# One DMA transpose of 1024 columns, or two of 512, in a recurrent attention and gated feed-forward kernel

## The chip, the core and the metric

The kernel runs on one core of a Trainium2 chip. The metric is the device time of one execution in microseconds (us). The engines named below are PE (TensorE: matmuls; PEld is its weight load), DVE (VectorE), ACT (ScalarE), POOL (GpSimd) and SP (SyncE, which here only issues DMAs). "SPq" is SP's queue of DMA issues: the time that SP spends on issuing.

## What is computed

Two stages, the second fed by the first. The first is a gated linear recurrence for each of 4 batches and 8 heads, over 768 positions with heads of 48:

```python
for t in range(S):
    state = alpha[:, :, t, :, None] * state + np.einsum('bhd,bhe->bhde', k[:, :, t], v[:, :, t])
    y[:, :, t] = np.einsum('bhd,bhde->bhe', q[:, :, t], state)
```

The second takes `x`, the output y with its heads side by side, 3072 rows of 384, and computes

```python
h = x @ w_in            # 384 -> 2048
g = h * np.cos(h)
return g @ w_out        # 2048 -> 384
```

Inputs and output are float32; the kernel multiplies in bfloat16.

## The kernel before

The 3072 rows are cut into 24 chunks of 128 positions, 6 for each batch. A chunk j goes through the recurrence in its parallel form: the logarithms of alpha are summed along the chunk by matmuls (`cums`, L162), the exponentials scale k and q (`scaled`, L208, by POOL or DVE) into the tile `kqb`, of which there are three slots, k in its first half and q in its second. Each half has 8 heads padded to 64 columns, so 512 columns a half and 1024 in all. Then k and q are transposed, so that the head's dimension lies along the partitions, into the tile `qkT` (128 partitions x 8 blocks x 128): blocks 0 to 3 hold k, 4 to 7 hold q, two heads a block. Scores (`scores`, L238) multiply blocks of both halves; a mask is applied (`mask_scores`, L246, on DVE); the state is updated (`state` L253, `ev_state` L260); outputs y come from scores and state (`outputs`, L275). The state matmuls read `kqb` itself, not its transpose.

The transpose has two forms. Chunks 0 to 8 use PE (`transposes`, L223) with a copy by DVE (`ev_transposes`, L231). Chunks 9 to 23 use a DMA transpose issued by SP (`transposes_dma`, L218 to L221): one instruction for all 1024 columns. `qkT` has six buffers.

The feed-forward stage of a chunk starts with y transposed too: on PE for some chunks (`x_transposes`, L300), by a DMA transpose of 384 columns on SP for 16 of them (`x_transposes_dma`, L296 to L298). Then come `ff1` (L313, 48 matmuls into `h_ps`), cosine on ACT (`act`, L323), the gate on DVE (`gate`, L329), `ff2` (L334) and a store.

The order of the work is written out by hand: one string, `ORDER` (L390), lists units such as `X17` (DMA transpose of chunk 17) or `K17` (k of chunk 17 scaled by POOL; `KD17` by DVE; `Q` and `QD` for q), and each unit emits its instructions on its engine in that order. Each engine works through its own list in order and waits for semaphores where it depends on others. So SP's list fixes the order in which loads of alpha, q, k and v (L111, L119), the weights, both kinds of transposes (L220, L298) and 16 of the 24 stores (L351) are issued; the other 8 stores are issued by ACT. Loads run ahead of their use by up to six chunks (`PF`).

In `ORDER` the transposes stand among the other units like this:

```python
"e7 A11 W9 k13 y10 E5 D10 et8 X12 u10 m11 eC8 eI8 Y11 A12 B10 st5 q13 v14 v12 G10 q15 yA11 D11 m12 B11 "
"V13 eI10 k18 u15 Y15 P_13 eC10 X16 bD16 x14 E9 A16 ss10 q18 S16 F14 m16 yA15 f_14 G14 X17 W13 Y16 QD18 "
"ss9 g_14 p_14 x15 e12 F15 a11 P_14 A17 yA16 W14 K18 bA17 uD16 V14 q19 m17 f_15 Y17 p_15 X18 A18 l11 G15 "
```

Of the kernel before, what the change touches and what calls it, by code (L numbers as in the profile page):

```python
# [16 lines left out]
def kernel(  # L17
# [10 lines left out]
    nc = tc.nc  # L28
# [5 lines left out]
    NP = H // 2  # L34
# [167 lines left out]
    def kq(j):  # L202
        return kqb[:, kq_slot.setdefault(j, len(kq_slot) % 3)]
# [13 lines left out]

    def transposes_dma(j):  # L218
        t = work.tile([C, 2 * NP, C], BF, tag="qkT", bufs=QB, name="qkT")
        nc.sync.dma_start_transpose(out=t, in_=kq(j).rearrange("s i h d -> s (i h d)"))  # L220
        qkT_t[j] = t  # L221

    def transposes(j):  # L223
# [138 lines left out]
    def on(f, *args):  # L362
# [12 lines left out]
        "K": on(scaled, 0, pool), "KD": on(scaled, 0, dve), "Q": on(scaled, 1, pool), "QD": on(scaled, 1, dve),  # L375
        "b": on(vcast, pool), "bA": on(vcast, act_e), "bD": on(vcast, dve),
        "X": transposes_dma, "T": transposes, "t": ev_transposes,
        "A": scores, "m": mask_scores, "S": state, "u": on(ev_state, pool), "uD": on(ev_state, dve),
        "Y": outputs, "y": on(ev_outputs, dve), "yA": on(ev_outputs, act_e),
# [71 lines left out]
```

## Time and profile before

| | |
|---|---|
| three runs | 192.05, 195.76 and 197.65 us; median 195.76 us |
| the profiled execution | 192.98 us, of which the span of the instructions is 191.3 us |
| granted TensorE clock | full in all 40 slices of the span |
| instructions | 5593 |
| matmuls of `ff1` (L320) and `ff2` (L340) | 70.3 and 69.7 us of PE's busy time, which overlaps itself |
| DMA transposes on SP | 15 of k and q (L220), 16 of y (L298) |
| DMA traffic | 35.74 MB in 117048 packets, mean 187 GB/s |
| SP's DMA queue (q1) | 115872 packets, 33.83 MB |
| ACT's DMA queue (q10) | 1152 packets, 1.57 MB, 8 stores |

The profile is one execution. A busy share of an engine is an average over the span. Lines of the timeline have the start and duration in us, the engine, the line of the kernel and the operation (out<-in); "x2" merges two neighbours, and brackets hold the idle time before the instruction and what ended it. "DMA to landing" is the time from the start of the issue on SP to the arrival of all data. In a window's DMA rows a digit is the mean busy share of the core's 16 DMA engines in a slice, in tenths, and GB/s is what they moved in it. Row "PE x ... [0.82 <-DVE g_sb L332]" reads: PE had nothing to do for 0.82 us, ended by DVE's result.

### The profile page before, as it was taken

What the parts mean: (1) busy time and instruction counts of PE and PEld (TensorE: products, weight loads), DVE (VectorE), ACT (ScalarE), POOL (GpSimd) and SP (SyncE); (2) the same over time, 40 slices, a digit from 0 to 9 for tenths busy, and PEclk for the clock granted to TensorE, in tenths of its full rate; (3) what the DMA queues carried; (4) which work ended last, traced back from release to release, by engine and by line L of the source; (5) the groups of instructions that cost most, each with busy time, mean ns of one, the idle gap of its engine ahead of it and who ended that gap; (6) DMA issues with size and microseconds to landing.
All of it is one profiled execution on the core that took longest, in us unless ns stands there. A gap on an engine that the chain in (4) does not pass through costs nothing.

```text
span 191.3 us, 5593 instructions
## 1 busy us (share of the span) xinstructions
PE 179.5 (94%) x2380; PEld 134.3 (70%) x2380; DVE 136.5 (71%) x181; ACT 119.7 (63%) x150; POOL 56.4 (30%) x85
## 2 busy tenths in 40 slices
PE   7988789999979999999999999899989999999992
PEld 2435568887758687887698858586857868877771
DVE  5024998888859787578768875877678978685371
ACT  2146588662768875458786988888676536326341
POOL 5042334135916130860246123402022244110000
PEclk9999999999999999999999999999999999999999
DMA  6999999999999896999999999989999998612122
GB/s 141 206 233 208 258 313 286 343 335 166 234 222 175 207 207 120 213 154 197 201 245 146 218 129 213 150 180 183 202 212 181 158 232 165 150 21 64 42 82 82
DMA packets 117048, 35.74 MB, mean 187 GB/s; under 512 B 110368, under 2 KB 115488, under 8 KB 117024
## 3 DMA queue, kind: packets, MB, share of 16 engines
q1 hardware_dynamic: 115872, 33.83, 88.4%
q10 hardware_dynamic: 1152, 1.57, 2.4%
q8 instruction: 18, 0.29, 0.7%
q14 instruction: 6, 0.05, 0.1%
HBM read 25.17 MB, written 4.72 MB: 156 GB/s over the span
## 4 chain that ended last, share of the span: by engine, by line
PE 67%; DMA 8%; SPq 8%; DVE 6%; ACT 4%; issue 3%; POOL 2%; DVEq 0%; POOLq 0%; ACTq 0%
PE o_ps L340 26%; PE h_ps L320 23%; PE w_ps L360 6%; SPq L220 4%; DMA qkT<-kqb 3%; PE A_ps L243 3%; DMA k_sb<-in_k_dram 2%; SPq L119 2%; DMA q_sb<-in_q_dram 2%; PE cum L167 2%; DVE g_sb L332 2%; SPq L298 2%; PE y_ps L285 2%; POOL kqb L210 2%; PE y_ps L282 1%
## 5 line engine op out<-in xcount | busy, mean ns | idle before, releaser
L326 ACT ACTIVATE c_sb<-h_ps,halfpi 128x1024 bf16<-128x1024 f32 x48 | 53.4, 1113 | 39.6 <-PE h_ps L320 38.0
L332 DVE TENSOR_TENSOR g_sb<-h_ps,c_sb 128x1024 bf16<-128x1024 f32 x48 | 58.5, 1220 | 19.4 <-ACT c_sb L326 18.5
L320 PE MATMUL h_ps<-xT,w 128*128 128x128 bf16 x1152 | 70.3, 219 | 0.7 <-DVE xT L309 0.4
L340 PE MATMUL o_ps<-w,g_sb 128*128 128x384 bf16 x384 | 69.7, 326 | 0.0
L320 PEld LDWEIGHTS <-w 128*128 128x128 bf16 x1152 | 65.8, 98 | 3.9 <-issue 0.6
L340 PEld LDWEIGHTS <-g_sb 128*128 128x128 bf16 x384 | 34.9, 98 | 21.0 <-issue 1.0
L248 DVE TENSOR_TENSOR A_sb<-A_ps,mask_f 128x1024 bf16<-128x1024 f32 x24 | 29.3, 1221 | 7.2 <-PE A_ps L243 7.1
L210 POOL TENSOR_TENSOR kqb<-k_sb,icpl 128x384 bf16<-128x384 f32 x18 | 18.6, 1034 | 22.8 <-DMA k_sb<-in_k_dram 10.6
L145 ACT ACT_TABLE_LOAD x18 | 23.1, 1283 | 1.1 <-PEq L435 0.8
L268 POOL TENSOR_TENSOR ub<-sc,Em 128x384 bf16<-128x384 f32 x10 | 8.6, 862 | 42.5 <-DVE sc L265 42.5
L210 POOL TENSOR_TENSOR kqb<-q_sb,cpl 128x384 bf16<-128x384 f32 x15 | 15.0, 1001 | 20.7 <-DMA q_sb<-in_q_dram 20.6
L360 PE MATMUL w_ps<-warm 128*128 128x512 bf16 x60 | 15.8, 406 | 1.3 <-DVE warm L58 1.3
L184 ACT ACTIVATE icpl<-cum 128x768 f32<-128x768 f32 (+1 forms) x13 | 10.0, 766 | 6.9 <-PE cum L167 6.9
L152 ACT ACTIVATE lnab<-a_sb 128x768 bf16<-128x768 f32 x12 | 10.2, 851 | 3.8 <-DMA a_sb<-in_alpha_dram 3.7
L184 ACT ACTIVATE cpl<-cum 128x768 f32<-128x768 f32 (+1 forms) x13 | 9.9, 762 | 3.7 <-PE cum L174 3.7
L210 DVE TENSOR_TENSOR kqb<-q_sb,cpl 128x384 bf16<-128x384 f32 x9 | 5.5, 607 | 9.0 <-ACT cpl L184 8.0
L285 PE MATMUL y_ps<-vpb,A_sb 128*128 128x48 bf16 x192 | 11.2, 183 | 0.4 <-DVE A_sb L248 0.4
L360 PEld LDWEIGHTS <-warm 128*128 128x128 bf16 x60 | 5.8, 103 | 7.9 <-issue 2.1
L285 PEld LDWEIGHTS <-A_sb 128*128 128x128 bf16 x192 | 9.7, 96 | 1.9 <-DVE A_sb L248 0.8
L243 PE MATMUL A_ps<-qkT 48*128 48x128 bf16 x192 | 9.5, 218 | 1.4 <-DVE A_sb L248 0.6
L282 PE MATMUL y_ps<-ub,qkT 128*128 128x96 bf16 x80 | 9.7, 204 | 0.6 <-POOL w L104 0.5
L265 DVE TENSOR_TENSOR sc<-U_ps,ub 128x384 f32<-128x384 f32 x16 | 8.8, 549 | 1.9 <-PE U_ps L257 1.9
(51 smaller groups left out, 132.3 us busy)
## 6 DMA issues: line engine op xcount, KB each, us to landing
q_sb<-in_q_dram SPq DMA_DIRECT2D x24, 192.0 KB, 4.7
a_sb<-in_alpha_dram SPq DMA_DIRECT2D x12, 384.0 KB, 4.9
k_sb<-in_k_dram SPq DMA_DIRECT2D x24, 192.0 KB, 4.7
v_sb<-in_v_dram SPq DMA_DIRECT2D x24, 192.0 KB, 4.3
w1f<-in_moe_w_in_dram SPq DMA_DIRECT2D x4, 768.0 KB, 6.9
w2f<-in_moe_w_out_dram SPq DMA_DIRECT2D x4, 768.0 KB, 9.1
out_dram<-o_sb SPq DMA_DIRECT2D x16, 192.0 KB, 2.9
out_dram<-o_sb ACTq DMA_DIRECT2D x8, 192.0 KB, 3.0
```

The source lines that it names most:

```text
L145: act_e.preload_act_table_set(nm)
L184: act_e.activation(out=d[g][:, c : c + n], in_=cum_of(g)[:, c : c + n, 0:HD], func=AF.Exp, scale=scale)
L210: eng.tensor_tensor(out=kq(j)[:, which, :, 0:D], in0=d.pop(j), in1=s[j // 2][:, j % 2].rearrange("s (h d) -> s h d", h=H), op=ALU.mult)
L243: nc.tensor.matmul(t[:, ACOL[h]], qkT_t[j][rows, h // 2], qkT_t[j][rows, NP + h // 2], start=True, stop=True)
L248: dve.tensor_tensor(out=t, in0=A_ps.pop(j), in1=mask_f.unsqueeze(1).to_broadcast([C, H, C]), op=ALU.mult)
L282: nc.tensor.matmul(t[:, 2 * p : 2 * p + 2], qT[:, NP + p], ub_t[prev(j)][:, p], start=True, stop=False, skip_group_check=True)
L285: nc.tensor.matmul(t[:, h], A[:, ACOL[h]], vp(j)[:, h], start=f, stop=True, skip_group_check=True)
L320: nc.tensor.matmul(t[:, f], w1[:, kk, ft * C : (ft + 1) * C], x_t[j][:, kk], start=(kk == 0), stop=(kk == 2))
L326: act_e.activation(out=t, in_=h_ps[j, half], func=AF.Sin, bias=halfpi, scale=1.0)
L332: dve.tensor_tensor(out=t, in0=h_ps.pop((j, half)), in1=c_t.pop((j, half)), op=ALU.mult)
L340: nc.tensor.matmul(o_ps[j][:, 0:DM], g_t[j, half][:, f], w2[:, half * HF + f], start=(o_n[j] == 0), stop=(o_n[j] == NF - 1))
L360: nc.tensor.matmul(w_t[0], warm[:, 0:C], warm, start=True, stop=True)
```

## The change

Each DMA transpose of scaled k and q is issued as two: k's 512 columns into blocks 0 to 3 of `qkT`, then q's 512 into blocks 4 to 7. Both are issued by SP, one right after the other, at the place in SP's list where the one stood. `ORDER` isn't touched, and the transposes of y and those on PE are as before. Each half waits for its own operand; the matmuls of the scores wait for both.

```diff
     def transposes_dma(j):
         t = work.tile([C, 2 * NP, C], BF, tag="qkT", bufs=QB, name="qkT")
-        nc.sync.dma_start_transpose(out=t, in_=kq(j).rearrange("s i h d -> s (i h d)"))
+        for i in range(2):
+            nc.sync.dma_start_transpose(out=t[:, i * NP : (i + 1) * NP], in_=kq(j)[:, i].rearrange("s h d -> s (h d)"))
         qkT_t[j] = t
```

## The prediction, made before the changed kernel ran

> **What bounds the kernel now.** I read the page first, then the idle time of PE, then the order of time on SP's queue, then the DMA rate in short windows.
>
> ```profile
> PE 179.5 (94%) x2380; PEld 134.3 (70%) x2380; DVE 136.5 (71%) x181; ACT 119.7 (63%) x150; POOL 56.4 (30%) x85
> PE 67%; DMA 8%; SPq 8%; DVE 6%; ACT 4%; issue 3%; POOL 2%; DVEq 0%; POOLq 0%; ACTq 0%
> ```
>
> PE is the bound, but the chain leaves PE for 16% of the span and runs through SP's queue and its transfers. The rows of PE in order of time show where that surfaces:
>
> ```profile
> 121.34 0.50 PE L167 MATMUL cum<-lnab,tri 64*128 64x384 bf16 x4 [0.82 <-DVE g_sb L332]
> 141.68 0.50 PE L167 MATMUL cum<-lnab,tri 64*128 64x384 bf16 x4 [0.67 <-DVE g_sb L332]
> 153.38 0.40 PE L243 MATMUL A_ps<-qkT 48*128 48x128 bf16 x8 [0.32 <-DMA qkT<-kqb]
> ```
>
> From 60 to 185 us the named idle time of PE is only these 1.8 us. The first goes back to a load: DVE waited 1.51 us for k of chunk 17, which SP issued at 114.23. So PE has almost nothing to win, and loses as soon as SP is late. SP's queue around that place:
>
> ```profile
> 107.79 4.45 SPq L220 DMA_TRANSPOSE qkT<-kqb  x2
> 112.34 1.21 SPq L298 DMA_TRANSPOSE xT<-y_sb  x1
> 113.60 0.57 SPq L119 DMA_DIRECT2D q_sb<-in_q_dram  x1
> 114.23 0.57 SPq L119 DMA_DIRECT2D k_sb<-in_k_dram  x1
> 114.85 2.34 SPq L119 DMA_DIRECT2D v_sb<-in_v_dram  x2
> 117.23 0.80 SPq L119 DMA_DIRECT2D k_sb<-in_k_dram  x1
> 118.13 3.15 SPq L220 DMA_TRANSPOSE qkT<-kqb  x1
> 121.38 1.20 SPq L298 DMA_TRANSPOSE xT<-y_sb  x1
> ...
> 123.78 1.42 SPq L220 DMA_TRANSPOSE qkT<-kqb  x1
> ```
>
> Start and duration stand in front. One instruction follows another within 0.1 us. From 57 to 165 us all of SP's gaps over 0.2 us add up to about 4 us (the largest at 60.6, 79.4, 143.1 and 162.9). This queue issues every load, transpose and most stores in a fixed order, so a longer instruction makes all behind it later.
>
> Its durations hold two things. The groups of the two transposes:
>
> ```profile
> L220 SPq DMA_TRANSPOSE qkT<-kqb x15: 1382/1933/3420, 67.6 to 161.4; - x15
> DMA to landing us min/median/max: 3.3/4.4/6.0
> L298 SPq DMA_TRANSPOSE xT<-y_sb x16: 1179/1202/2120, 61.8 to 174.3; - x16
> DMA to landing us min/median/max: 2.3/2.7/4.9
> ```
>
> Three blocks of 128 columns cost 1.18 us at least, eight cost 1.38: (1.38 - 1.18) / 5 = 0.04 us a block over a fixed 1.06. The cost is nearly all fixed, and the change pays it twice. What lies above 1.4 is mostly not a wait for data: the POOL rows end k of chunk 13 at 97.4 and of 16 at 116.1, well before 99.98 and 118.13 where their transposes begin and take 3.42 and 3.15 us. (The table of waits puts some of it down to POOL and DVE writing other chunks.) It is a queue waiting to drain: from 98 to 102 the DMA engines moved 203 to 238 GB/s with a backlog. I call these drain-limited. The third view, 85 to 90 us in 40 slices:
>
> ```profile
> DMA  9999999970000999999999999999999997799999
> GB/s 309 302 297 292 265 178 119 59 23 17 16 18 18 215 287 289 261 256 263 263 258 264 215 190 182 188 178 188 262 258 289 284 180 138 143 160 132 197 203 241
> ```
>
> The transpose of chunk 11 is issued at 85.87; the engines are empty until slice 13 (86.6), then move at about 260 GB/s. So 0.75 us of the fixed part pass before the first byte.
>
> **The change, part by part.**
>
> *Issue on SP.* Fifteen instructions of 8 blocks become thirty of 4. One half costs 1.06 + 4 x 0.04 = 1.22; I take 1.25, with a gap of 0.08 before the next (the rows' gaps are 0.05 to 0.10), so 2.58 for a pair. Against the undisturbed single of 1.38 to 1.59 this is +1.0 to +1.2. Against the drain-limited singles (2.18 to 3.42; chunks 10, 13, 14, 15, 16, 18, 19) it is +0 to +0.4, since the second fixed part passes while the backlog drains. If nothing is absorbed, 15 x (1.25 + 0.08) = 20 us are added to the queue; if all is, none. I take the rows one by one, below.
>
> *Landing.* The second half lands 1.33 us after the first is issued, plus 2.3 (3 blocks) to 2.5 (4 blocks, 0.2 us a block by the two minima): 3.8, against 3.3 to 3.8 undisturbed and 4.4 in the median. So scores come at the same time to 0.5 later, counted from the issue of the first half.
>
> *Waits.* k's half waits for k only. That gains only where SP stood at a transpose with q alone missing. By the rows of POOL and DVE this is chunk 20 alone: q ends at 147.32, SP was free at 147.0; gain 0.3 us. For others, where k is scaled after q (11, 12, 13, 15, 16, 19, 21, 23), k first cannot gain at all. The order of instructions on every engine stays as it was, and PE, DVE, ACT and POOL execute the same list, so they get no work more; PE's scores wait for both halves.
>
> *DMA engines.* On the ACT queue 8 stores are 1152 packets, 144 each: 128 rows and 16 more. Taking 16 more from each load and store on SP's queue, 22496 of 115872 packets remain for the 31 transposes: 168 blocks x 128 = 21504, and 32 for each instruction. The change adds 15 x 32 = 480, 0.4%; at the mean share that is below 1 us in all, and I put it at 0.3, inside the issue term. Bytes don't change. Should the halves not overlap on the DMA engines, an empty 0.3 us (0.75 less the 0.45 in which the first half moves) stands in each undisturbed pair; it is in the landing above.
>
> *Who becomes late.* PE's delay is not the sum of SP's delays but the largest lateness of a deadline beyond its slack. Before 107.8: chunk 9's extra goes into the gaps at 73.9 and 79.4; those of 10 to 12 (about 2.5 us) come before five loads that took 0.87 to 2.32 instead of 0.57, and are mostly absorbed; their transposes land 2.6 to 4.2 us before the scores that need them. I carry 0.3.
> - Chunks 14 and 15: 4 halves take 4 x 1.25 + 3 x 0.08 = 5.2 instead of 4.45, +0.75. With the carry, k of 17 is issued 1.0 later; DVE is already waiting for it, so PE is +0.9 at 121.3.
> - Chunk 17 (1.42 to 2.58): +1.15. The transpose of y for chunk 15 behind it landed at 128.4, and its matmuls began at 128.62: slack 0.2. SP is 1.0 + 1.15 = 2.1 late, less slack 0.2 and the 0.9 that PE is late already: +1.0, PE 1.9.
> - Chunk 18: landed 133.5, scores at 133.51, no slack; it is drain-limited behind the alpha load at 127.17. SP 2.1 and 0 to 0.4 late: PE +0.3, so 2.2.
> - Chunks 19 and 20 also have no slack (143.83 against 143.85, and the 0.32 above), but loads from 134 to 137 can take back some 0.7 and chunk 20 the 0.3: covered by the 2.2.
> - Chunks 21 to 23 landed 1.7 to 3.1 us ahead of their scores; up to +1.1 each fits in that and in PE's lateness. Then PE runs alone to the end.
>
> Sum: +2.2 us. The profiled execution took 192.98 us (span 191.3 and 1.7 around it), which makes 195.2. It is a quick one: the median of the three runs is 195.76, 1.4% above, so against that I expect **198.0 us**, +1.1%. Measurements of this kernel tell a change from none at about 2%.
>
> A rule of the Trainium skill speaks against the change: "DMA: Bandwidth & Descriptors", section Bandwidth, wants DMAs batched, with small ones dominated by their descriptors; its fitted fixed cost of about 2.0 us (section on the anatomy of one DMA, measured on another issuing path) would, if paid in series fifteen times, be an estimated 30 us. The trace agrees that a fixed part rules (2.3 us to land 3 blocks, 3.3 for 8), but most of it is latency that overlaps: the pair at 107.79 was issued 2.3 us apart and landed 5.2 and 4.2 us after issue. A fixed cost in series is rival 3 below.
>
> **The rivals.**
> 1. *The queue becomes the bound, and the time is clearly longer.* Nothing drain-limited is absorbed: the long rows are the instruction's own time, and each pair adds a full 1.3. From chunk 10 to 19 ten pairs add 13 us; less 3 us of gaps and of load slack at the five loads, SP is 10 late at chunk 20, where there is no slack: +9 to +10, 205. Half absorbed gives +5, 201. It decides from 3.9 us of SP lateness at 153 on. For it: SP has few gaps, and at 128 to 129 the DMA engines moved little (0 to 131 GB/s) while chunk 18's instruction still took 3.06. Against: the loads at 113.60 and 114.23, with an empty queue ahead, took 0.57 each, and the two right behind them 2.34, so a queue that has to drain does stretch rows.
> 2. *Hidden, or a little gain.* Halves land sooner than one whole because the first moves while the second is issued; drain-limited pairs land up to 0.5 sooner, and chunks 18 to 20 are such. PE can win back at most its 1.8 us: 194.0 to 196.5. For it: median landing of 4.4 against 3.8 worked out above. Against: k of chunk 17 and the y transposes stand behind the pairs.
> 3. *Serial halves.* A second transpose starts only when the first has landed: each pair lands 2.3 to 2.5 later than now, and the lateness carries on from chunk 17 to 20, three of them without slack: 3 x 2.4 = +7 at least, +12 with the queue's own: 203 to 208. Against: chunks 14 and 15 above were in flight together. This is what the skill's fixed cost in series would come to.
>
> **How the numbers follow.** Forecast (+1 to +3.9): 0.42, within 2%. Rival 1: 0.32, slower. Rival 2: 0.18, nearly all within 2%; I leave 0.04 for faster by over 2%, which no row supports beyond the spread of the runs (192.05 to 197.65). Rival 3: 0.08, slower. Thus faster 0.04, same 0.56, slower 0.40. The likeliest case's own range is 196.5 to 199.7. The range to hold 8 in 10 reaches from rival 2's lower end to the half-absorbed rival 1 and some way past it: 193.5 to 204.
>
> **What would show it.** Thirty instructions at the transposes' line of 1.2 to 1.3 us where undisturbed, with drain-limited pairs hardly over their old sum; k of chunk 17 issued about 1 us later relative to PE; PE's idle time at cum near 121 grown to some 1.7, and a new one ahead of h_ps near 129; chunks 21 to 23 without any. I am wrong if a half costs well under 1 us (then rival 2), if pairs behind loads grow by 1.3 as well (rival 1), or if the second half's landing is over 3 us (rival 3).

## The result and the profile after

The changed kernel took 203.05 us (median of 4 runs, 202.35 to 204.86), the kernel before 194.9 us (median of 4, 192.05 to 197.65): a ratio of 1.053, 95% interval 1.038 to 1.068. A ratio here leaves out slow executions, over 1.5% above the quickest of their kernel, and a median takes all, so the two need not divide out exactly. The time lies inside the stated range, near its upper end. The forecast of no change that can be told was wrong: the change costs 5%, and what happened is the first rival.

The profiled execution took 202.35 us with a span of 200.6, 9.3 more than before. From the page, PE's row and the chain's shares by engine:

```profile
PE 180.6 (90%) x2380; PEld 134.8 (67%) x2380; DVE 136.9 (68%) x181; ACT 119.8 (60%) x150; POOL 56.3 (28%) x85
PE 39%; DMA 21%; SPq 21%; DVE 5%; ACT 5%; POOL 4%; issue 3%; ACTq 0%; POOLq 0%; DVEq 0%
```

Every engine does the work that it did before, in almost the same busy time. The chain, two thirds on PE before, is now as long on SP's queue and its transfers (42%) as on PE (39%). Seven of the fifteen rows of PE with over 0.15 us of idle time ahead of them (lines after 220 of the kernel have moved down by one):

```profile
86.69 2.85 PE L321 MATMUL h_ps<-xT,w 128*128 128x128 bf16 x48 [0.96 <-DMA xT<-y_sb]
...
104.82 1.50 PE L321 MATMUL h_ps<-xT,w 128*128 128x128 bf16 x24 [0.61 <-DVE g_sb L333]
...
125.12 0.50 PE L167 MATMUL cum<-lnab,tri 64*128 64x384 bf16 x4 [1.47 <-DVE g_sb L333]
...
128.92 2.84 PE L321 MATMUL h_ps<-xT,w 128*128 128x128 bf16 x48 [0.49 <-DMA xT<-y_sb]
136.18 1.51 PE L321 MATMUL h_ps<-xT,w 128*128 128x128 bf16 x24 [2.75 <-DMA xT<-y_sb]
...
157.14 1.50 PE L321 MATMUL h_ps<-xT,w 128*128 128x128 bf16 x24 [0.53 <-DVE g_sb L333]
161.87 0.40 PE L244 MATMUL A_ps<-qkT 48*128 48x128 bf16 x8 [0.59 <-DMA qkT<-kqb]
```

All of PE's idle stretches over 0.15 us from 60 us on add up to 10.1 us, where they were 1.8 before: those 8.3 us more are most of the 9.3. Set against the same matmul before, PE is 0.5 us late at 60 us, where nothing is changed yet, 1.65 at 86.7, 3.1 at 119.3, 3.8 at 125.1, 4.7 at 128.9, 7.6 at 136.2, 8.5 at 161.9 and 9.7 at the last scores. It is a loss in many small steps and one large one. SP's queue around the place shown before:

```profile
110.17 6.45 SPq L221 DMA_TRANSPOSE qkT<-kqb  x4
116.71 1.22 SPq L299 DMA_TRANSPOSE xT<-y_sb  x1
117.98 0.57 SPq L119 DMA_DIRECT2D q_sb<-in_q_dram  x1
118.61 0.57 SPq L119 DMA_DIRECT2D k_sb<-in_k_dram  x1
119.22 1.71 SPq L119 DMA_DIRECT2D v_sb<-in_v_dram  x2
120.98 0.95 SPq L119 DMA_DIRECT2D k_sb<-in_k_dram  x1
122.03 4.30 SPq L221 DMA_TRANSPOSE qkT<-kqb  x2
126.44 1.21 SPq L299 DMA_TRANSPOSE xT<-y_sb  x1
...
128.80 2.68 SPq L221 DMA_TRANSPOSE qkT<-kqb  x2
131.52 0.58 SPq L352 DMA_DIRECT2D out_dram<-o_sb  x1
132.20 2.64 SPq L299 DMA_TRANSPOSE xT<-y_sb  x1
```

Chunks 14 and 15 take 6.45 us for 4.45, chunk 16 takes 4.30 for 3.15 and chunk 17 takes 2.68 for 1.42. The first two of these rows had been called drain-limited, and grew all the same. Over all fifteen, the rows of these transposes on SP grew from 31.5 to 44.5 us, with 15 gaps more, 14.2 us in all. The group, and its landing:

```profile
L221 SPq DMA_TRANSPOSE qkT<-kqb x30: 1190/1265/2992, 69.5 to 173.4; - x30
DMA to landing us min/median/max: 2.5/3.3/5.6
```

### The profile page after: what moved, and what is told of

It is laid out like the page before. It is cut to its first block, busy times and chain, and to the rows that moved or that the text cites. A ratio compares the mean times of both kernels' runs of the same rounds, so it can differ in the third digit from the quotient of the medians.

```text
span 200.6 us, 5628 instructions
## 1 busy us (share of the span) xinstructions
PE 180.6 (90%) x2380; PEld 134.8 (67%) x2380; DVE 136.9 (68%) x181; ACT 119.8 (60%) x150; POOL 56.3 (28%) x85
## 3 DMA queue, kind: packets, MB, share of 16 engines
q1 hardware_dynamic: 116352, 33.83, 87.0%
## 4 chain that ended last, share of the span: by engine, by line
PE 39%; DMA 21%; SPq 21%; DVE 5%; ACT 5%; POOL 4%; issue 3%; ACTq 0%; POOLq 0%; DVEq 0%
PE h_ps L321 16%; PE o_ps L341 16%; DMA k_sb<-in_k_dram 11%; SPq L119 10%; SPq L221 7%; DMA qkT<-kqb 6%; DVE g_sb L333 2%; POOL kqb L210 2%; DMA a_sb<-in_alpha_dram 2%; ACT c_sb L327 2%; SPq L111 2%; SPq L299 1%; PE A_ps L244 1%; DMA xT<-y_sb 1%; DVE sc L266 1%
## 5 line engine op out<-in xcount | busy, mean ns | idle before, releaser
L244 PEld LDWEIGHTS <-qkT 48*128 48x128 bf16 x192 | 5.8, 94 | 7.4 <-issue 5.0
(51 smaller groups left out, 136.1 us busy)
```

The costliest lines, as they stand in the source:

```text
L244: nc.tensor.matmul(t[:, ACOL[h]], qkT_t[j][rows, h // 2], qkT_t[j][rows, NP + h // 2], start=True, stop=True)
```

## The experiments

Theory A: a transpose costs about 1.25 us of SP's in-order queue whatever its width, and all that stands behind it is late by that. Theory B: the cost is that of one more DMA in flight. Theory C: two halves move their data worse on the DMA engines. In the table each ratio is that of the kernel to the kernel before, run on the same chip, with its 95% interval.

| run | median us | ratio |
|---|---|---|
| e1, whole, and a tiny copy behind each | 198.26 | 1.030 (1.024 to 1.037) |
| e2, split, SP's stores issued by ACT | 204.28 | 1.060 (1.052 to 1.068) |
| e3, whole, SP's stores issued by ACT | 198.15 | 1.023 (1.011 to 1.036) |
| e4, split, q first | 202.73 | 1.053 (1.046 to 1.060) |
| e5, chunks 9 to 15 split | 198.19 | 1.028 (1.019 to 1.037) |
| e6, chunks 16 to 23 split | 196.86 | 1.018 (1.010 to 1.026) |
| e7, in four quarters | 239.59 | 1.247 (1.239 to 1.256) |
| e9, split, v loads issued by ACT | 209.53 | 1.081 (1.070 to 1.093) |
| e10, whole, v loads issued by ACT | 203.05 | 1.052 (1.041 to 1.063) |
| e11, split, v loads left out | 194.20 | 1.008 (1.003 to 1.013) |
| e12, whole, v loads left out | 191.15 | 0.989 (0.981 to 0.997) |

**e1: queue time without a transpose.** The tile `tiny` is allocated at the start (not shown).

```diff
         nc.sync.dma_start_transpose(out=t, in_=kq(j).rearrange("s i h d -> s (i h d)"))
+        nc.sync.dma_start(out=tiny[:, 8 * j : 8 * j + 8], in_=warm[:, 0:8])
```

> The whole transpose of 1024 columns stays; a copy of 16 bytes in each of 128 partitions follows each of the 15 on SP's queue, needed by nobody. Theory A (what the second half costs is its issue time on SP's in-order queue): a plain DMA takes 0.4 to 0.6 us to issue there, so 15 of them add 6 to 9 us to the queue where the halves added 14: about half of the loss, ratio 1.02 to 1.03, 198 to 201 us. Theory B (what costs is one more DMA in flight, with its completion and its place among the eight completion semaphores that SP's DMAs take in turn): as much as the split, ratio 1.05, 203 us or more. Theory C (two halves move their data worse on the DMA engines than one whole): no loss, ratio 1.00 to 1.01.

```profile
L222 SPq DMA_DIRECT2D tiny<-warm x15: 582/591/659, 70.4 to 170.9; - x15
```

15 x (0.59 + 0.08) = 10 us on the queue, moving next to nothing and read by nobody, cost 5.8 us (198.26 against 192.45). The split's 14.2 us cost 10.3 against the same kernel before (202.73 in e4). That is 0.6 and 0.7 us of time for a us of queue. As many DMAs as in the split, at little over half of its price, speak against B; any loss at all without halves speaks against C as the whole cause. The 5.8 us are not all waiting: in the profile PE's idle stretches from 60 us on are 5.0 us (1.8 before), and behind the longest of them, which ends at 133.5, the granted clock of PE averages 0.61 from 134 to 138 us, where the kernel before has the full clock throughout.

**e4: the other order.** `for i in (1, 0)`, q's half first.

> Split as in the changed kernel, q's half issued ahead of k's. Theory A: the number and length of the instructions is the same, so the loss is the same: ratio 1.045 to 1.06, 202 to 205 us. If the order of the halves mattered (a half that waits for its operand at the head of the queue), it would move by over 1%.

1.053, as the split. That k goes first gains and costs nothing measurable.

**e7: the dose.** Four transposes of 256 columns, as an edit of the kernel before.

```diff
-        nc.sync.dma_start_transpose(out=t, in_=kq(j).rearrange("s i h d -> s (i h d)"))
+        for i in range(2):
+            for p in range(0, NP, 2):
+                nc.sync.dma_start_transpose(out=t[:, i * NP + p : i * NP + p + 2],
+                                            in_=kq(j)[:, i, 2 * p : 2 * p + 4].rearrange("s h d -> s (h d)"))
```

> Each of the 15 transposes issued as four of 256 columns. Theory A: 45 instructions more than before at 1.2 us and 0.08 between them are 57 us more on a queue that has 4 us of gaps; the first 14 us cost 10 and the rest costs about all of it: 235 to 250 us, ratio 1.22 to 1.30. If the cost were by bytes or packets, it would stay under 1.08.

```profile
L222 SPq DMA_TRANSPOSE qkT<-kqb x60: 1169/1244/2906, 68.4 to 212.4; - x60
```

Half the width, and a median of 1.24 us again. 45 instructions more are 45 x (1.24 + 0.08) = 59 us of queue, and the kernel is 47 us longer. The bytes are the same. But not all of the 47 us is time spent waiting. The granted clock, by the pages of e7 and of the kernel before:

```profile
PEclk9999999999999999979979859788997995899999
PEclk9999999999999999999999999999999999999999
```

The clock averaged 0.935, and PE's busy time for the same matmuls grew from 179.5 to 195.6 us. PE's idle time from 60 us on is 31.4 us, for 1.8 before. So some 30 us are waiting and 16 are slower matmuls. The second was in no sum, so that the result fell within the expected 235 to 250 us was in part luck.

**e5 and e6: where.** `if j <= 15:` (e5) or `if j >= 16:` (e6) splits, else whole.

> Only the seven transposes of chunks 9 to 15 are split. Theory A: SP's queue grows by the 6 us that these pairs grew by in the changed kernel, and PE can be late by what is left of it behind them, less slack: +2.5 to +4.5 us, ratio 1.013 to 1.025. If the loss came from one place only (chunk 17's pair and the y transpose behind it, 2.9 us in the profile after), 1.00 to 1.01.

> Only the eight transposes of chunks 16 to 23 are split, the other part. Theory A: the queue grows by 8 us, and the deadlines without slack (chunks 17 to 20) lie here: +4 to +7 us, ratio 1.02 to 1.037; both parts together make about the whole loss, 1.05.

+2.8% and +1.8%, together 4.6 of the 5.3. The first part costs more and the second a little less than expected. The two intervals overlap, so that the first part costs more than the second is not shown. It is shown that the seven pairs of chunks 9 to 15, which the prediction let nearly vanish in gaps and stretched loads, cost 2.8% by themselves (1.9% at the low end of the interval).

**e2, e3, e9, e10: relief by ACT, which failed as a test.** In e2 and e3 the unit `ss` calls `on(store, act_e)`. In e9 and e10 `load` issues v from chunk 6 on from ACT. (e3 and e10 are the controls, with the whole transpose.)

> The split kernel with the 16 stores that SP issued issued by ACT instead. Theory A: SP's queue gets back 16 x 0.6 = 9 to 10 us of the 14 that the split added, so most of the loss goes: ratio 1.00 to 1.02, 195 to 199 us, unless the stores hold ACT up. Theory B: the number of DMAs is the same, so 1.04 to 1.05. Theory C: the transposes are the same, so 1.05.

> The kernel before with its 16 SP stores issued by ACT: the control for the run above. Theory A: PE had only 1.8 us of named idle time to win in the profile before, so 0.985 to 1.00 (192 to 195 us). If ACT is hurt by issuing stores it shows here, above 1.00. Theories B and C: 1.00.

> The split kernel with the loads of v from chunk 6 on (18 of them) issued by ACT. Unlike the stores they wait for no result, so ACT is held up for the issue alone. Theory A (issue time on SP's queue): SP gets 18 x 0.65 = 12 us back of the 14 added: ratio 1.00 to 1.02, 193 to 197 us. Theory C (halves move worse on the DMA engines): 1.05.

> The kernel before with the same 18 loads issued by ACT: the control for the run above, and a candidate for a faster kernel. Theory A: SP's lateness was already on the chain before, worth at most 1.8 us of PE's idle time: ratio 0.985 to 1.00, 190 to 193 us; above 1.00 if ACT is hurt.

All four expectations by A were missed: the two splits, 1.060 and 1.081, were not relieved at all, and both controls were slower than the kernel before, 1.023 and 1.052. Taken alone, e2 is nearer to what B and C gave for it. The idle time of PE in e10 names v:

```profile
72.37 0.21 PE L286 MATMUL y_ps<-vpb,A_sb 128*128 128x48 bf16 x2 [1.57 <-POOL vpb L104]
105.41 0.33 PE L258 MATMUL U_ps<-vpb,kqb 128*128 128x96 bf16 x4 [3.52 <-DVE vpb L104]
153.06 0.33 PE L258 MATMUL U_ps<-vpb,kqb 128*128 128x96 bf16 x4 [3.10 <-POOL vpb L104]
```

I read it so: a load takes its turn in ACT's list, behind activations that wait for PE, and is issued later than SP would have issued it; the thirteenth load of v is issued at 97.0 us in e10, at 90.5 in the kernel before. In e3 PE waits 2.6 us for `qkT`; why was not settled. Against their own controls the splits cost 1.060/1.023 = 1.036 and 1.081/1.052 = 1.028, less than 1.053, as A has it; but with controls so disturbed this shows little by itself. Neither version is of use.

**e11 and e12: relief without another engine.** The loads of v from chunk 6 on are left out and chunk 5's v is used, kept in a tile `v_keep` that is allocated at the start (not shown), so the outputs of those chunks are not the reference's.

```diff
         b, c = CH[j]
-        d[j] = inpool.tile([C, H, D], FP, tag=nm, name=nm)
+        if nm == "v_sb" and j > 5:
+            d[j] = v_keep
+            return
+        d[j] = v_keep if nm == "v_sb" and j == 5 else inpool.tile([C, H, D], FP, tag=nm, name=nm)
```

> The split kernel without the 18 loads of v from chunk 6 on; the v of chunk 5 is used for them. This gives SP's queue back 18 x 0.64 = 11.5 us without giving another engine work. Theory A: the queue is about as long as before the change, so the cost of the split nearly vanishes: 0.99 to 1.015 against the kernel before, and no more than 1.015 against the control below. Theory C (halves move worse on the DMA engines, whatever the queue's length): still 1.04 to 1.05 above the control.

> The kernel before without the same 18 loads (chunk 5's v for them): the control for the run above. Theory A: PE has at most 1.8 us to win, 0.985 to 1.00.

```profile
PE cum L171 <- DVE g_sb L337: 0.8, 2, 0.6
PE h_ps L325 <- DVE g_sb L337: 0.4, 1, 0.4
PE o_ps L345 <- DVE o_sb L105: 0.2, 1, 0.2
```

These are all of PE's waits in e11 from 60 us on, in us, with how many and the longest. With 18 loads less on the queue the same split costs 194.20/191.15 = 1.016 (1.019 by the two ratios, give or take 0.009 by their intervals), not 1.053, and PE's idle stretches in e11 add up to 1.4 us, not 10.1. It did not quite vanish: it came out just above the 1.015 that I had allowed, though within the noise of it. Leaving the loads out takes bytes off the DMA engines too, so this pair alone does not separate queue from traffic; e1, which adds queue time and next to no traffic, does. That the whole gains only 1.1% here says that a shorter queue is worth little to the kernel before; no faster version came out of this.

**e8 and e13: the transposes by themselves.** These kernels leave out all of the computation; their output is zeros. Each is one execution. They issue transposes of a zeroed tile on SP in phases, each phase on lines of its own; one of them, shortened:

```python
for r in range(R):          # behind a backlog: whole, then in another phase a pair
    for i in range(4):
        nc.sync.dma_start(out=loads[i], in_=k[r % B, :, i * C : (i + 1) * C, :].rearrange("h s d -> s h d"))
    nc.sync.dma_start_transpose(out=one, in_=flat(0, 8))
    nc.sync.dma_start_transpose(out=other, in_=flat(0, 1))      # its start shows the end of the one before
    nc.sync.dma_start_transpose(out=one[:, 0:1], in_=flat(0, 1))    # waits until the whole has landed
```

> Not the attention kernel: SP's transposes measured by themselves (the output is zeros). In turn: transposes of 1, 3, 4 and 8 blocks alone on an empty queue, pairs of 4 and 4 alone, a whole and then a pair behind four loads of 192 KB with PE idle, and wholes alone while PE works through 1100 matmuls. As the prediction has it (a queue that drains stretches the instruction): behind the loads the whole takes 2 to 3 us and the pair about as much, within 0.4; alone with PE at work 1.4 to 1.6 each. By the rival found in the trace after (what stretches a transpose to 2 to 3 us is one DMA engine taken for 1.0 to 1.6 us by a packet of 16 KB of PE's instructions): behind the loads with PE idle the pair takes some 1.1 to 1.2 more than the whole; alone with PE at work some of the 15 take 2 us and more, about one for each 128 matmuls that pass.

Groups of e8: count, then duration on SP in ns (min/median/max), then when, with the landing under some. L68 is 1 block, L72 4 and L74 8, each alone; L76 and L77 are a pair, nothing ahead of it; L81 is the whole behind four loads; L86 and L87 are the pair there. PE is idle in all of them.

```profile
L68 SPq DMA_TRANSPOSE one<-src x5: 1094/1096/1197, 1.4 to 10.5; - x5
...
L72 SPq DMA_TRANSPOSE one<-src x5: 1189/1190/1191, 24.3 to 34.1; - x5
...
L74 SPq DMA_TRANSPOSE one<-src x5: 1232/1232/1232, 36.5 to 48.8; - x5
DMA to landing us min/median/max: 3.0/3.0/3.1
...
L76 SPq DMA_TRANSPOSE one<-src x5: 1190/1264/1265, 51.9 to 62.3; - x5
L77 SPq DMA_TRANSPOSE one<-src x5: 1264/1264/1267, 53.1 to 63.6; - x5
DMA to landing us min/median/max: 2.5/2.5/2.5
...
L81 SPq DMA_TRANSPOSE one<-src x5: 1597/1723/2044, 67.7 to 99.4; - x5
...
L86 SPq DMA_TRANSPOSE one<-src x5: 1388/1519/1669, 107.7 to 141.6; - x5
L87 SPq DMA_TRANSPOSE one<-src x5: 1258/1265/1267, 109.1 to 143.0; - x5
```

One block costs SP 1.10 us and eight cost 1.23. Behind the backlog the whole takes 1.72 in the median and the pair 1.52 + 0.05 + 1.27 = 2.84: +1.1, as on an empty queue (2 x 1.26 + 0.05 against 1.23 is +1.3). The first half takes most of the stretch, and the second its full fixed time behind it. So a backlog hides next to nothing of the second half. It does not make rows of 3 us either: the longest is 2.04.

What does is in the windows of the trace. Before, from 118 to 122 us, where chunk 16's transpose took 3.15:

```profile
DMA  9999999999999999999999999999999916100000
GB/s 169 150 169 177 190 158 179 161 182 173 202 186 204 341 173 217 194 175 173 194 208 198 195 189 187 201 214 182 177 179 122 56 28 17 10 13 15 17 17 18
...
q8 instruction: 1, 0.02, 2.1%
```

In the last seven slices 10 to 18 GB/s move, at a mean busy share of the 16 DMA engines below a tenth, where mostly 150 to 220 moved before. I read that as one engine being behind while the others have nothing left. The row q8 counts one packet of 16 KB of instructions. It occupied its engine from 119.3 for 1.35 us. Of the ten rows of SP over 2 us between 57 and 160 in the kernel before, nine overlap such a packet for over 0.9 us (chunks 10, 13, 15, 16, 18 and 19 among them), and the tenth, chunk 14, for its last 0.1. This was a likeness of times, so e13 put backlog and PE's work (3200 matmuls) together. In e8, with PE at work and no backlog, one of the 15 wholes took 2.10 us on SP and the others at most 1.26, fewer than the "some" expected there; what came late was their landing.

> SP's transposes by themselves again (the output is zeros): ten wholes and ten pairs, each behind four loads of 192 KB, with PE idle, and the same with PE working through 3200 matmuls. If the backlog alone makes the long rows of the kernel (2.2 to 3.4 us), they appear with PE idle too. If a DMA engine taken by a packet of PE's instructions makes them, then with PE idle no whole takes over 2.1 us, and with PE at work some take 2.3 to 3.4, each at a time when such a packet is under way. In both, if nothing is absorbed, a pair takes 1.0 to 1.2 us more than a whole in the mean.

L73 is the whole with PE idle, L88 with PE at work; then two windows with PE at work, of a whole that took 2.75 us and of one that took 2.00:

```profile
L73 SPq DMA_TRANSPOSE one<-src x10: 1516/1639/1955, 3.7 to 74.2; - x10
...
L88 SPq DMA_TRANSPOSE one<-src x10: 1435/1848/2802, 166.4 to 249.8; - x10
```

```profile
184.59 2.75 SPq L88 DMA_TRANSPOSE one<-src  x1
...
202.60 2.00 SPq L88 DMA_TRANSPOSE one<-src  x1
```

```profile
q1 hardware_dynamic: 3671, 0.73, 114.2%
q8 instruction: 1, 0.02, 1.6%
...
q1 hardware_dynamic: 3341, 0.65, 116.3%
```

The window of 184 to 188 holds an instruction packet, that of 202 to 205 holds none. With PE idle no whole took over 1.96 (2.04 in e8). With PE at work four of ten took 2.34 to 2.80, and each of the four overlapped such a packet; none of the other six did. A packet doesn't always do it: three second halves of pairs that overlapped one took 1.26 or 1.27 and only landed late, 3.5 to 3.9 us after issue. The pair cost 2.80 us in the mean against 1.68 for the whole with PE idle, 2.95 against 2.04 with PE at work: +1.1 and +0.9, with a gap of 0.05 more. So the rows well over 2 us are those of a DMA engine held by a packet, on top of a backlog. Such packets fall on whatever is being issued, and give little cover.

## Why the prediction was wrong

*The step that failed* is the one on SP's issue: "against the drain-limited singles (...) it is +0 to +0.4, since the second fixed part passes while the backlog drains." By the profile after, the pairs of those seven chunks grew by 0.73 (chunk 10), 0.37 (13), 2.0 (14 and 15 together), 1.15 (16), -0.23 (18) and 0.67 (19). That is 4.7 us in all, where the list of deadlines has 0.75 for 14 and 15, up to 0.4 for 18, nothing for 16 and 19, and one carry of 0.3 for all that comes ahead of 14. By e8 and e13, 0.9 to 1.1 is the rule, and 18 is luck: its row before overlapped an instruction packet, its pair after did not. The same belief stands in a second place, and there it weighed more: "and are mostly absorbed (...) I carry 0.3." Chunk 13's first half was issued at 102.56 where the whole had been at 99.98; less the 0.5 that this execution was late before any change, 2.1 us were carried, not 0.3; the five loads had taken back 0.6 of the 2.7 that SP was late ahead of them. Chunk 17's pair began 4.5 us late by the same reckoning (1.0 foretold), chunk 20's 7.6. I had read a long row as a wait that would hide new work, without asking what it waited for; the trace of before already held a hint, in the row q8 and in the DMA rate that falls to 10 to 18 GB/s.

*The fixed cost was right*: 1.22 us for a half, worked out from the minima of 1.18 and 1.38, is 1.19 to 1.27 in e8 and 1.27 in the median after. The whole, however, costs 1.23 alone, not 1.38. Pairs that were undisturbed before and after (chunks 9, 11, 12, 17, 21, 23) grew by 0.9 to 1.3, for the +1.0 to +1.2 foretold. One reading behind it was off: in e8 the first data move 1.1 us after the issue starts, not 0.75, so those at 86.6 us in the kernel before can have been of the load issued at 85.20.

*Landing was right for undisturbed pairs*: in e8 a half lands 2.5 us after its issue, and the second one 1.31 + 2.5 = 3.8 us after the first is issued, as worked out; chunks 9, 11, 12 and 17 have 3.75 to 3.94 after the change. Over all fifteen pairs it is 3.75 to 6.3, with a median of 4.6, against 4.4 for the whole before. That the scores come at most 0.5 later, counted from the first issue, holds in the median.

*The gain by k's half going first* did not show: chunk 20's pair, which was to win 0.3, grew by 1.9 with an instruction packet in its second half, and e4 without that order is no slower.

*Chunk 9 was wrong for a second reason.* I let its extra go into the gaps. The first new idle time of PE, 0.96 at 86.7, comes from there: with chunk 9's pair, SP's gap of 1.5 us before the y transpose at 80.94 was nearly gone, loads were still being moved, and that transpose landed 5.2 us after its issue instead of 2.4. A gap in the queue was also time in which the DMA engines emptied. e5 puts 2.8% on chunks 9 to 15.

*k of chunk 17* was foretold 1.0 us later relative to PE, with idle time of some 1.7 at cum: DVE waited 2.7 us for it instead of 1.5, PE 1.47 instead of 0.82. *The y transpose behind chunk 17* was the right place with the wrong size: +1.0 foretold, and PE's idle time there was 2.75. It was issued 6.3 us later than before, took 2.64 instead of 1.20 as an instruction packet of 1.65 us had begun at 132.8, and landed at 136.1. That such a packet falls there is chance. e6, without the first seven pairs, has a wait of 2.0 for a y transpose too.

*Chunks 18 to 20 and 21 to 23* were to be covered by PE's own lateness. They were not quite: 0.2, 0.6, 0.2 and 0.4 us of idle time at the scores of 19, 20, 21 and 23, as SP stayed as late as PE or later.

*The rivals.* Rival 1, the queue as the bound with nothing absorbed, was the result, at 203 for the 201 to 205 that I gave; I had set it at 0.32. Its deciding point, 3.9 us of lateness at chunk 20, was passed with 7.6. Not all of its account holds: a pair adds 0.95 us in the mean (14.2 for fifteen), not a full 1.3. Rival 2 is out: PE won nothing back. So is rival 3, though the sign that I had set for it, a second half that lands over 3 us after its issue, did come for seven of the fifteen: the second half lands 0.65 us behind the first in the median, 2.3 or more behind it for chunk 23 alone, while in series it would be 2.3 to 2.5 each time. The 480 packets more that I counted are 480 on SP's queue (116352 against 115872), and of no account.

*What stays open*: the last 1.6% of the split in e11, why the controls with stores on ACT are slower, what lowers PE's clock in e1 and e7, and how much of the stretch by an instruction packet grows when there are twice as many transposes for it to fall on.

## What to carry to other kernels

Price a DMA by what it holds of its queue: where a queue issues without gaps and the bound engine has little slack, a fixed 1.25 us more, fifteen times, cost this kernel most of itself, and narrower pieces cost the same each. Don't book new work under an instruction's long row before you know what made it long; if what it waited for is an event of another engine, splitting the instruction doesn't shorten the wait and the new part comes on top. And the queue's order is shared: moving an issue to another engine takes it out of the reach of that order, and made things worse here twice.

## What the runs showed of the hardware that was not expected

A DMA transpose's time on SP hardly knows its width: 1.10 us for 128 columns, 1.19 for 512, 1.23 for 1024, alone on the queue, while a plain copy of 192 KB takes 0.58.

PE's instructions come over DMA engines too, and the profile counts their packets among those of the 16 engines that carry the kernel's data. In e13, 25 packets of 16 KB came for 6402 matmuls and weight loads, one for each 256, none while PE was idle; each took 0.9 to 1.7 us of an engine's time. On an empty queue in e8, seven of 15 transposes landed 0.5 to 1.6 us late while PE was at work, and behind a backlog the issue itself was held. The Trainium skill, "Runtime: NRT & Kernel Launch", section Instruction fetch mechanics, says that instructions are refilled in blocks of 16 KiB, 256 of them, over a DMA queue of the sequencer's own, and that this is mostly hidden. The size and number agree with these runs. Hidden it was from PE, but not from the transfers beside it.
